# A gated attention unit with a token mixer: the small last group projected within a run of large ones, a reordered opening, and an earlier small output at the end

## The chip, the cores and the metric

The kernel runs on one core of a Trainium2 chip. The metric is the device time of one execution in microseconds. A core has TensorE (PE; its weight loads are shown as PEld), VectorE (DVE), ScalarE (ACT), GpSimd (POOL) and SyncE (SP, which here only issues DMAs), and 16 DMA engines that serve the queues of all of them.

## What is computed

Two layers, for 8 batches of 3200 rows; `u` and `v` have 256 columns, `z` has 64.

```
scores = z @ z^T / 3200                     # per batch, 3200 x 3200, symmetric
x      = u * (relu(scores)^2 @ v)           # 3200 x 256
wq, wk = x @ w_q, x @ w_k                   # 3200 x 64 each
mixed  = (wq @ wk^T / 8) @ x                # 3200 x 256
out    = relu(mixed) @ w_out                # 3200 x 256
```

There is no softmax, so `wk^T @ x` (64 x 256, the "heads") can be summed up first and `mixed` is `wq` times it.

## The kernel before

**Tiles and groups.** The 3200 rows of a batch are 25 tiles of 128. They form seven groups of output rows: six large ones of 512 and a small last one of 128 (`LASTG`, index 6). For a group and each of the 25 tiles, `scores` (L265) makes a 128 x 512 block of scores; two blocks form a pair, which takes one buffer of two banks in PSUM. `first_stage` reads the pair with relu and a scale into `g` (ACT L287 or DVE L291), `second_stage` squares `g` into `at` in FP16 (ACT L307 or POOL/DVE L310). `second_product` (L353) multiplies `at` with `v` and accumulates in four banks, `acc00` to `acc11`: half of the group's rows by half of the contraction, so that two matmuls of 64 rows run beside each other. Since the scores are symmetric, some blocks are not made again but transposed by DMA (`tt`, `ttl`; L332).

**Gate and second layer.** When a half of a group is done, `gate` copies one bank (ACT or DVE, L370), adds the other (DVE, L371), which frees the accumulators, and POOL multiplies with `u` (L390). A DMA transposes `x` (L402); `projections` (L419) gives `wq` and `wk`, a DMA transposes `wk` (L438), and `heads` (L457) sums `wk^T @ x` over the seven groups of a batch (`hacc`, on DVE). Then per group `mix` (L485), relu into `rt` (ACT L508 or DVE L510), `proj` (L520, the product with `w_out`: 8 matmuls for a large group, 2 for the small one), `proj_out` (DVE L542 or ACT L547) and a store (SP, L548). This second layer of a batch runs between the accumulations of the next one.

**Two score buffers.** Scores, projections, heads, mixes and output projections all take their PSUM from one pool of two buffers (`ps_tile`). Whoever opens a third waits until the first is read.

**The order.** A planner written into the kernel (L582 to L1055) fixes the order of all instructions. It keeps a clock for PE, DVE, ACT and POOL, adds an assumed duration for each instruction (`give`), decides by them which engine takes a pass (`choose`, `squares`, with the constants `BIAS`, `SPARE`, `MORE`, `LATE`, `UNTIL`), and gives PE the next thing that the clocks allow: an accumulation, a pair of scores, or an "extra" of the second layer. `heads_known` releases the mixes of a batch in three steps, groups 0 and 1, groups 2, 3 and 6, and groups 4 and 5. `use_mix` gathers large groups in twos (`PAIRED`) before it asks for a projection; the small group asks for one of its own.

**The opening** is by hand (L988 to L1015): POOL makes the identity, SP and ACT load `z` of batch 0 in four pieces (`ZCH`: 4, 6, 7 and 8 tiles), 28 matmuls on the identity fill PE's first microseconds, three pieces are cast to FP16 twice over (two engines each), turned on PE (L132) and copied to `zT` (L139); POOL loads four pieces of `v`. The fourth piece of `z` is cast on DVE when the planner's clock stands at 8.6 and turned at 10.0. Up to 24 us on that clock pairs may be split into halves on two engines (`UNTIL`).

**The end** (L1102 to L1135) finishes the last batch: seven output projections, of which the small one comes last, its store behind those of group 5.

Of the kernel before, what the change touches and what calls it, by code (L numbers as in the profile page):

```python
# [16 lines left out]
def kernel(  # L17
# [95 lines left out]
    def cast_first(c):  # L113
        n0, nn = ZCH[c]
        casts = [
            (nc.vector.tensor_copy, nc.scalar.copy),
            (nc.scalar.copy, nc.gpsimd.tensor_copy),
            (nc.gpsimd.tensor_copy, nc.vector.tensor_copy),
            (nc.vector.tensor_copy, nc.vector.tensor_copy),
        ][c]  # L120
        for half, cast in enumerate(casts):
            cast(out=zd0[:, n0 : n0 + nn, half, :], in_=z32[n0][:])

    def turn_first(c):
        n0, nn = ZCH[c]
        if c < 3:
            tp = acc_tile((c + 1) // 2 % 2, c % 2, "ztp", FP16)
        else:
            open_slot()
            tp = pps.tile([P, 4 * W], FP16, tag="ps", name="ztp")  # L130
        for i in range(nn):
            nc.tensor.transpose(  # L132
                tp[:, ts(i, P)], zd0[:, n0 + i, :, :].rearrange("p a k -> p (a k)"), ident
            )
        clock[PE] += 0.055 * cold() * nn
        ready = clock[PE] + FROM_PE
        on_act = max(clock[ACT], ready) < max(clock[DVE], ready)
        copy = nc.scalar.copy if on_act else nc.vector.tensor_copy
        copy(out=zT[0][:, ds(n0 * P, nn * P)], in_=tp[:, 0 : nn * P])  # L139
        z_at[c] = give(ACT if on_act else DVE, ready, 0.16 + 0.07 * nn)  # L140
        if c == 3:
            close_slot(z_at[c])

    def warm(n):
        for _ in range(n):
            nc.tensor.matmul(out=idle[:, 0:P], lhsT=ident[:], rhs=ident[:], start=True, stop=True)
# [113 lines left out]
    def scores(p):  # L260
        assert len(ztimes) >= 4 * tiles[2 * p + 1][0] and p_chunk(p) in z_at, (p, clock, len(ztimes), z_at)
        sc = ps_tile("sc")
        for h, (b, gi, ti) in enumerate(tiles[2 * p : 2 * p + 2]):
            gs, gw = starts[gi], widths[gi]
            nc.tensor.matmul(  # L265
                out=sc[:, h, 0:gw],
# [13 lines left out]
    def first_stage(p, sc, ways):  # L280
# [4 lines left out]
        for (hs, w), on_act in zip(parts, ways * 2):  # L285
            if on_act:
                nc.scalar.activation(  # L287
                    out=g[:, hs, 0:w], in_=sc[:, hs, 0:w], func=RELU, scale=GSCALE
                )
            else:  # L290
                nc.vector.tensor_scalar(  # L291
                    out=g[:, hs, 0:w], in0=sc[:, hs, 0:w], scalar1=0.0,
# [235 lines left out]
    def proj_out(b, gi, banks, ways, stores=None, at=0):  # L528
# [3 lines left out]
        else:  # L532
            fo = pg.tile([P, 2, W], FP32, tag="fo", name="fo", bufs=2)
# [64 lines left out]
    PAIRED = [0, 1, 2, 3, 4, 5]  # L598
# [48 lines left out]
    def cold():  # L647
        return 2.0 if clock[PE] < 8.4 else 1.0
# [3 lines left out]
    UNTIL = 24.0  # L652
# [8 lines left out]

    def use_pair():
# [7 lines left out]
        if clock[PE] < UNTIL and max(a + 0.57, d + 0.68) + SPLIT < min(a + 1.03, d + 1.2):  # L670
            ways = [a < d, a >= d]
            done = max(give(ACT, ready, 0.57), give(DVE, ready, 0.68))
        else:
            ways = [choose(a, d)]
            done = give(ACT, ready, 1.03) if ways[0] else give(DVE, ready, 1.2)
# [4 lines left out]
    def squares():  # L680
        while pending and pending[0][0] <= clock[PE] + 0.3:
# [6 lines left out]
            if clock[PE] < UNTIL and max(a + 0.57, c + 0.97) + SPLIT < min(a + 1.06, c + 1.9):  # L688
                ways = [a < c, a >= c]
                done = max(give(ACT, ready, 0.57), give(POOL, ready, 0.97))  # L690
# [78 lines left out]
    def heads_known(b):  # L769
        t = clock[PE]  # L770
        for i, gis in enumerate(([0, 1], [2, 3, LASTG], [4, 5])):
# [3 lines left out]
    def use_mix(b, gi):  # L775
# [14 lines left out]
        if gi in PAIRED:  # L790
            if len(mixed_at) == 2:
                add_extra(done + 0.5, "proj", use_projs)
        else:
            add_extra(done + 0.5, "proj", use_projs)

    def use_projs():
        some = mixed_at[:]
        mixed_at.clear()
        banks = []
        clock[PE] += 0.22  # L800
        for _, b, gi in some:
# [4 lines left out]
            banks.append((b, gi, ps, clock[PE] + FROM_PE))  # L806
        for i, (b, gi, ps, ready) in enumerate(banks):
            project_out(b, gi, ps, ready)

    def project_out(b, gi, ps, ready):  # L810
# [6 lines left out]
        stored.append(1e9)  # L817

        def landed(t, i=len(stored) - 1):
            stored[i] = t  # L820
# [9 lines left out]
    V0 = 56  # L830
    V1 = 11

    def batch_begun(b, t):
        if b + 1 < B:
            t0 = max(t + 6, Z0)
            if b == 0:
                nc.gpsimd.memset(zn[:, 0 : NT + 2 : NT + 1, :], 0.0)
# [32 lines left out]
    SPARE = 0.3  # L870
    MORE = 3.0
    BIAS = 0.2
    XDUE = 5.0
    XWAIT = 2.0
    LATE = 0.3
# [92 lines left out]
    def calm_for(kind):  # L968
# [7 lines left out]
        if kind == "proj":  # L976
            n = len(mixed_at)
# [21 lines left out]
    clock[:] = [4.4, 4.75, 4.3, 7.0]  # L999
    for t, n0, nn in ((7.0, 0, 4), (18.0, 4, 8), (10.5, 12, 6), (14.0, 18, 7)):  # L1000
# [20 lines left out]
    while groups or work or current["left"]:  # L1021
# [10 lines left out]
                and (x[1] != "proj" or all(t + 2.0 <= now for t in stored[-2:][: len(mixed_at)]))  # L1032
# [5 lines left out]
        if extra and extra[1] == "proj":  # L1038
            room = slots[len(mixed_at) - 1] <= now
# [84 lines left out]
    for gi in range(NG):  # L1124
# [3 lines left out]
        elif gi == LASTG - 1:  # L1128
            mixed(last, LASTG, LASTG)
        if gi == 0:  # L1130
# [3 lines left out]
        else:  # L1134
            projected(last, gi, [(True, nc.sync, widths[gi] // P)])  # L1135
# [30 lines left out]
```

## Time and profile before

| | us |
|---|---|
| runs of the kernel before | 777.76, 778.35, 779.88 (median 778.35) |
| the profiled execution | 776.21 |
| its span in the trace | 774.4 |
| PE busy in it | 762.9 (99%) |
| DVE, ACT, POOL busy | 518.8, 548.5, 603.2 |

A row of a group gives the line, the engine, the operation, what is written from what, the count, then after the bar the busy time in us and the mean of one in ns, and after the second bar the idle time in front of it with its releasers. A row of the timeline begins with start and duration in us; a number in brackets is the idle time ahead of it. A row of the windows gives the stretch, then busy time and count for PE, PEld, DVE, ACT and POOL, the granted clock, the DMA engines' busy share and GB/s. A row of waits gives who waited for whom, the total in us, how often, and the longest. A row of DMA issues gives the size and the microseconds from issue to landing.

### The profile page before, as it was taken

Reading aid. Unit: us, or ns where it says so; the run is one execution under the profiler, and the core shown is the slowest. Engines: PE = TensorE matmul, PEld = TensorE weight load, DVE = VectorE, ACT = ScalarE, POOL = GpSimd, SP = SyncE. Lnnn points to the kernel's source line nnn. Section 1 sums busy time; section 2 is a strip of 40 time slices with the busy share of each in tenths; the row PEclk is TensorE's granted clock in tenths of the full one; section 3 lists DMA queues with packets and bytes.
Section 4 is the critical chain, followed back from the end, with each engine's and each line's share of the span. In section 5 each row is a group of like instructions: output and inputs, shape, how many; then the busy total and the mean of one; then the engine's idle time right before and its main releaser. Section 6 shows DMA issues by size and latency. Waiting matters only on the chain.

```text
span 774.4 us, 28287 instructions
## 1 busy us (share of the span) xinstructions
PE 762.9 (99%) x12410; PEld 673.8 (87%) x12410; DVE 518.8 (67%) x550; ACT 548.5 (71%) x635; POOL 603.2 (78%) x510
## 2 busy tenths in 40 slices
PE   7999999999999999999999999999999999999996
PEld 6889999889898888988889888998889988898884
DVE  6687687766676566766667657675676756765545
ACT  6686777577666677776877767787587777677734
POOL 7789688888787679867879878778866778878941
PEclk9999999999999999999999999999999999999999
DMA  7999999999999979999999988999999998889745
GB/s 184 157 167 184 133 191 164 169 196 200 187 219 186 198 200 189 174 188 185 207 186 185 201 199 149 198 171 174 229 195 189 161 237 168 162 176 206 144 91 190
DMA packets 307115, 141.10 MB, mean 182 GB/s; under 512 B 285744, under 2 KB 288432, under 8 KB 306992
## 3 DMA queue, kind: packets, MB, share of 16 engines
q1 hardware_dynamic: 300224, 123.13, 82.6%
q0 software_dynamic: 6624, 15.98, 14.8%
q8 instruction: 97, 1.59, 0.9%
q10 hardware_dynamic: 144, 0.20, 0.1%
q14 instruction: 26, 0.21, 0.1%
HBM read 59.64 MB, written 26.21 MB: 111 GB/s over the span
## 4 chain that ended last, share of the span: by engine, by line
PE 94%; DVE 2%; DMA 2%; POOL 1%; issue 0%; ACT 0%; POOLq 0%; DVEq 0%; SPq 0%
PE acc L353 69%; PE sc L265 13%; PE fo L520 6%; PE qk L419 3%; PE qk L457 2%; PE mx L485 1%; DMA v_sb<-in_v_dram 1%; DVE g L291 1%; POOL x_sb L390 1%; DMA z<-in_z_dram 0%; DVE fo L542 0%; DMA xT_sb<-x_sb 0%; DVE both L371 0%; POOL at L310 0%; DVE both L370 0%
## 5 line engine op out<-in xcount | busy, mean ns | idle before, releaser
L353 PE MATMUL acc<-v_sb,at 64*128 64x256 f16 x7344 | 500.8, 269 | 1.3 <-POOL at L310 0.8
L310 POOL TENSOR_TENSOR at<-g 128x1024 f16<-128x1024 f32 (+2 forms) x232 | 414.4, 1799 | 84.8 <-DVE g L291 46.3
L353 PEld LDWEIGHTS <-at 64*128 64x128 f16 x7344 | 403.1, 94 | 52.8 <-issue 7.2
L291 DVE TENSOR_SCALAR g<-sc 128x1024 f32<-128x1024 f32 (+1 forms) x294 | 341.2, 1181 | 107.5 <-PE sc L265 97.4
L307 ACT ACTIVATE at<-g 128x1024 f16<-128x1024 f32 (+1 forms) x250 | 251.3, 1021 | 27.3 <-DVE g L291 24.1
L287 ACT ACTIVATE g<-sc 128x1024 f32<-128x1024 f32 (+2 forms) x184 | 180.5, 984 | 76.6 <-PE sc L265 72.0
L265 PE MATMUL sc<-zT 64*128 64x512 f16 x924 | 186.5, 375 | 2.4 <-DVE g L291 1.4
L390 POOL TENSOR_TENSOR x_sb<-both,u_sb 128x512 f16<-128x512 f32 (+1 forms) x112 | 135.6, 1215 | 63.7 <-DVE both L371 62.9
L353 PE MATMUL acc<-v_sb,tt 64*128 64x256 f16 x2272 | 162.7, 269 | 0.0
L353 PEld LDWEIGHTS <-tt 64*128 64x128 f16 x2272 | 126.6, 94 | 11.1
L371 DVE TENSOR_TENSOR both<-acc,both 128x512 f32<-128x512 f32 (+1 forms) x104 | 69.7, 671 | 23.6 <-ACT both L370 18.7
L265 PEld LDWEIGHTS <-zT 64*128 64x128 f16 x924 | 61.9, 94 | 7.9 <-issue 4.0
L370 ACT COPY both<-acc 128x512 f32<-128x512 f32 (+1 forms) x63 | 36.0, 571 | 45.7 <-PE acc L353 41.8
L542 DVE TENSOR_SCALAR fo<-fo 128x1024 f32<-128x1024 f32 (+2 forms) x30 | 33.1, 1116 | 42.7 <-PE fo L520 42.6
L508 ACT ACTIVATE rt<-mx 128x1024 f16<-128x1024 f32 (+1 forms) x46 | 42.5, 926 | 12.8 <-PE mx L485 12.7
L520 PE MATMUL fo<-wo,rt 128*128 128x256 f16 x400 | 49.5, 274 | 0.1
L370 DVE COPY both<-acc 128x512 f32<-128x512 f32 (+1 forms) x41 | 27.3, 665 | 31.3 <-PE acc L353 28.5
L520 PEld LDWEIGHTS <-rt 128*128 128x128 f16 x400 | 36.4, 98 | 10.7 <-issue 6.5
L433 ACT CAST qk<-qk 128x512 f16<-128x512 f32 (+1 forms) x45 | 24.4, 542 | 25.3 <-PE qk L457 22.7
L547 ACT ACTIVATE fo<-fo 128x1024 f32<-128x1024 f32 (+2 forms) x28 | 24.4, 871 | 23.7 <-PE fo L520 23.0
L472 DVE TENSOR_TENSOR ha<-qk,ha 128x512 f32<-128x512 f32 x37 | 25.5, 688 | 16.7 <-ACT qk L433 16.2
L419 PE MATMUL qk<-xT_sb,wqk 64*128 64x256 f16 (+1 forms) x404 | 32.8, 266 | 0.0
(47 smaller groups left out, 276.4 us busy)
## 6 DMA issues: line engine op xcount, KB each, us to landing
u_sb<-in_u_dram SPq DMA_DIRECT2D x48, 512.0 KB, 4.7
out_dram<-fo SPq DMA_DIRECT2D x46, 512.0 KB, 4.2
v_sb<-in_v_dram POOLq DMA_DIRECT2D x35, 320.0 KB, 6.1
zn<-in_z_dram POOLq DMA_DIRECT2D x7, 400.0 KB, 5.9
tt<-at SPq DMA_TRANSPOSE x143, 4.5
u_sb<-in_u_dram SPq DMA_DIRECT2D x8, 128.0 KB, 3.0
out_dram<-fo SPq DMA_DIRECT2D x8, 128.0 KB, 3.5
out_dram<-fo SPq DMA_DIRECT2D x4, 256.0 KB, 2.6
```

The costliest lines, as they stand in the source:

```text
L265: nc.tensor.matmul(out=sc[:, h, 0:gw], lhsT=z_cols(b, h, ti * P, P), rhs=z_cols(b, h, gs, gw), start=True, stop=True,)
L287: nc.scalar.activation(out=g[:, hs, 0:w], in_=sc[:, hs, 0:w], func=RELU, scale=GSCALE)
L291: nc.vector.tensor_scalar(out=g[:, hs, 0:w], in0=sc[:, hs, 0:w], scalar1=0.0, scalar2=GSCALE, op0=AOP.max, op1=AOP.mult,)
L307: nc.scalar.square(out=out, in_=g[:, hs, 0:w])
L310: mul(out=out, in0=g[:, hs, 0:w], in1=g[:, hs, 0:w])
L353: nc.tensor.matmul(out=accs[half, r][:, ds((j % 2) * D, D)], lhsT=weights(b, gi, ti, j)[top(r), :], rhs=vs[b][top(r), ti, :], start=(first ...
L370: copy(out=both[:, 0 : n * D], in_=accs[half, 0][:, 0 : n * D])
L371: nc.vector.tensor_add(out=both[:, 0 : n * D], in0=accs[half, 1][:, 0 : n * D], in1=both[:, 0 : n * D])
L390: nc.gpsimd.tensor_mul(out=xs[b, gi][:, 0:n, :, r, :].rearrange("p n c d -> p (n c) d"), in0=both[:, 0 : n * D].rearrange("p (m d) -> p m ...
L419: nc.tensor.matmul(out=ps[:, r, 0 : n * P], lhsT=wqk[top(r), c, :, :].rearrange("p t h -> p (t h)"), rhs=xTs[b, gi][top(r), 0:n, c, :], st ...
L508: nc.scalar.activation(out=out, in_=part, func=RELU)
L520: nc.tensor.matmul(out=banks[r][:, ds(j * D, D)], lhsT=flat[:, ds((dc * n + j) * P, P)], rhs=wo[:, dc, :], start=(dc == 0 and j == 0), sto ...
```

## The change

Four things change.

1. **Runs of projections.** `RUNS` replaces `PAIRED`: groups 2, 3 and 6 are mixed and then projected in one go, the small group first. Its relu result and its output get small buffers of their own (`rtl`, `fol`), the sum of heads has one buffer instead of two, and the store of the small output no longer counts among those that hold the next projection back. Each output is read right behind its own projection in the order.
2. **The opening.** DVE clears the later home of `w_out` and the two padding tiles of `z`; the first matmuls run on that cleared tile (31 instead of 28, and none later). POOL asks for the first piece of `v` ahead of the identity and for the second right behind it. All four pieces of `z` are cast at once, the fourth by POOL and ACT; it is turned at 7.5 on the planner's clock. The first pair of scores goes to two accumulator banks (`first_pair`), split on ACT and DVE, and squared by ACT and POOL. The fourth piece of `v` is asked for at 7.5.
3. **The planner's constants.** Score passes are never split any more, squares only before 8 us; `SPARE` 0.3 to 0.1, `MORE` 3.0 to 0.6, `BIAS` 0.2 to -0.2, `XWAIT` 2 to 7, `LATE` 0.3 to 0.5, `V0` 56 to 48, `V1` 11 to 10. A smaller `MORE` lets DVE take squares, a negative `BIAS` prefers ACT for score passes and outputs.
4. **The end.** The small group is projected and stored ahead of group 5, its output read by ACT.

```diff
 def cast_first(c):
-            (nc.vector.tensor_copy, nc.vector.tensor_copy),
+            (nc.gpsimd.tensor_copy, nc.scalar.copy),
...
 def heads_out(b, gi, ps):
-            hacc[b] = psml.tile([P, 2, D], FP32, tag="ha", name="ha")
+            hacc[b] = psml.tile([P, 2, D], FP32, tag="ha", name="ha", bufs=1)
...
 def mix_out(b, gi, ps, by_act=True):
-            rts[b, gi] = prt.tile([P, 2, ND, HW], FP16, tag="rt", name="rt")
+            if gi < LASTG:
+                rts[b, gi] = prt.tile([P, 2, ND, HW], FP16, tag="rt", name="rt")
+            else:
+                rts[b, gi] = prt.tile([P, 1, ND, P], FP16, tag="rtl", name="rtl", bufs=1)
...
-    PAIRED = [0, 1, 2, 3, 4, 5]
+    RUNS = [[0, 1], [2, 3, LASTG], [4, 5]]
...
+    def first_pair():
+        produced[0] += 1
+        sc = scores(0, [acc_tile(0, r, "sc")[:] for r in range(2)])
+        clock[PE] += 0.22
+        ready = clock[PE] + FROM_PE
+        a, d = give(ACT, ready, 0.6), give(DVE, ready, 0.69)
+        free_at[0] = max(a, d)
+        g = first_stage(0, sc, [True, False])
+        for x, t in zip(tiles, (give(ACT, a, 0.63), give(POOL, d, 1.05))):
+            row_at[x] = t + 0.3
...
 def use_mix(b, gi):
-        if gi in PAIRED:
-            if len(mixed_at) == 2:
-                add_extra(done + 0.5, "proj", use_projs)
-        else:
+        if len(mixed_at) == len(next(x for x in RUNS if gi in x)):
             add_extra(done + 0.5, "proj", use_projs)

 def use_projs():
-        some = mixed_at[:]
+        some = sorted(mixed_at[:], key=lambda x: (x[2] < LASTG, x[2]))
...
-            banks.append((b, gi, ps, clock[PE] + FROM_PE))
-        for i, (b, gi, ps, ready) in enumerate(banks):
-            project_out(b, gi, ps, ready)
+            project_out(b, gi, ps, clock[PE] + FROM_PE)
...
-    make_identity(nc, ident)
+    blank = wo[:, 0, 0:P]
+    nc.vector.memset(blank, 0.0)
+    nc.vector.memset(zn[:, 0 : NT + 2 : NT + 1, :], 0.0)
     load_first_z()
     load_first_v(0, 4)
-    idle = acc_tile(0, 1, "warm")
-    warm(28)
-    cast_first(0)
-    cast_first(1)
-    cast_first(2)
+    make_identity(nc, ident)
     load_first_v(12, 6)
+    idle = acc_tile(1, 0, "warm")
+    warm(31)
+    for c in range(4):
+        cast_first(c)
     load_first_v(18, 7)
-    load_first_v(4, 8)
...
-    use_pair()
+    first_pair()
     use_pair()
     turn_first(2)
-    warm(5)
-    at_time(8.6, lambda: (cast_first(3), give(DVE, 8.6, 0.86)))
-    at_time(10.0, lambda: turn_first(3))
+    at_time(T3, lambda: turn_first(3))
+    at_time(V3, lambda: (load_first_v(4, 8), give(POOL, clock[PE], 0.6)))
...
-    for gi in range(NG):
+    for gi in range(LASTG):
...
         elif gi == LASTG - 1:
             mixed(last, LASTG, LASTG)
+            projected(last, LASTG, [(False, nc.sync, 1)])
```

More of the change, by code (lines that the diff above doesn't have):

```diff
@@ L136, in turn_first @@
         ready = clock[PE] + FROM_PE
-        on_act = max(clock[ACT], ready) < max(clock[DVE], ready)
-        copy = nc.scalar.copy if on_act else nc.vector.tensor_copy
+        ways = [(max(clock[e], ready) + t, e, t) for e, t in ((DVE, 0.16 + 0.066 * nn), (ACT, 0.17 + 0.105 * nn))]
+        _, engine, t = min(ways)
+        copy = nc.scalar.copy if engine == ACT else nc.vector.tensor_copy
         copy(out=zT[0][:, ds(n0 * P, nn * P)], in_=tp[:, 0 : nn * P])
-        z_at[c] = give(ACT if on_act else DVE, ready, 0.16 + 0.07 * nn)
-        if c == 3:
-            close_slot(z_at[c])
+        z_at[c] = give(engine, ready, t)
+        free_at[1] = max(free_at.get(1, 0.0), z_at[c])
     def warm(n):
         for _ in range(n):
-            nc.tensor.matmul(out=idle[:, 0:P], lhsT=ident[:], rhs=ident[:], start=True, stop=True)
+            nc.tensor.matmul(out=idle[:, 0:P], lhsT=blank, rhs=blank, start=True, stop=True)
         clock[PE] += 0.053 * cold() * n
@@ L669, in use_pair @@
         a, d = (max(clock[x], ready) for x in (ACT, DVE))
[L670 to L675, printed above, removed]
+        ways = [choose(a, d)]
+        done = give(ACT, ready, 1.03) if ways[0] else give(DVE, ready, 1.22)
         g = first_stage(p, sc, ways)
```

74 lines of the change are left out of this document (39 added, 35 removed).

## The prediction

> **What bounds the kernel now.** I read the page's busy shares first, then the windows by stage, then TensorE's own waits. Every number is of one profiled execution: 776.21 us, of which the span is 774.4; the median of the three runs shown is 778.35, so 2.14 us is put on top of a sum made against the profiled execution. A change of less than 0.3% (2.3 us) can hardly be told from none here; that is the bound of "same" below.
>
> ```profile
> span 774.4 us, 28287 instructions
> PE 762.9 (99%) x12410; PEld 673.8 (87%) x12410; DVE 518.8 (67%) x550; ACT 548.5 (71%) x635; POOL 603.2 (78%) x510
> ...
> 4.50:8.70 4.20, 2.83 (x33) 1.82 (x33) 3.47 (x6) 2.93 (x6) 4.16 (x7) 1.00 0.88 203
> 8.70:16.00 7.30, 5.99 (x90) 4.61 (x91) 6.15 (x9) 4.69 (x8) 5.75 (x5) 1.00 1.03 237
> 16.00:24.00 8.00, 7.49 (x117) 6.04 (x113) 6.09 (x8) 6.62 (x13) 7.10 (x7) 1.00 0.60 93
> 50.00:60.00 10.00, 9.10 (x146) 8.01 (x144) 8.59 (x9) 8.82 (x11) 8.15 (x9) 1.00 1.00 148
> 60.00:100.00 40.00, 40.00 (x687) 39.08 (x684) 28.37 (x31) 27.70 (x31) 32.31 (x29) 1.00 1.08 163
> ```
>
> TensorE is busy for 99% of the span, and busy time flatters it, since overlapping matmuls count as busy however slowly they are issued. The count in brackets shows the pace: from 60 to 100 us 687 matmuls start in 40 us, 17.2 per us. At that pace the 90 of 8.7 to 16 us are 5.2 us of work (2.1 lost), the 117 of 16 to 24 us are 6.8 (1.2 lost), the 146 of 50 to 60 us are 8.5 (1.5 lost). So apart from its fixed work this kernel can be made faster only in the opening, in the patch around 50 us, in the changes of matmul kind, and behind the last matmul.
>
> ```profile
> PE sc L265 <- DVE g L291: 1.4, 3, 0.7
> PE acc L353 <- POOL at L310: 0.8, 1, 0.8
> PE acc L353 <- DVE both L371: 0.2, 1, 0.2
> PEld L520 <- issue: 6.5, 31, 0.2
> ```
>
> TensorE's waits for other engines are few and short; the weight loads of the output projection (L520) stand idle 0.2 us on entry 31 times, whatever else goes on.
>
> **Part 1: the small group inside a run of two.** Before, each of the seven scheduled batches visits the output projection four times (16, 16, 2 and 16 matmuls); after, three times (16, 18, 16), as the changed program's instruction order shows: 28 entries become 21, with 400 matmuls in both. One small visit:
>
> ```profile
> L353 PE MATMUL acc<-v_sb,at 64*128 64x256 f16 x7344 | 500.8, 269 | 1.3 <-POOL at L310 0.8
> ...
> 188.45 1.42 PE L353 MATMUL acc<-v_sb,ttl 64*128 64x256 f16 x22
> 189.80 0.11 PEld L520 LDWEIGHTS <-rt 128*128 128x128 f16 x2 [0.21 <-issue]
> 189.80 0.39 PE L520 MATMUL fo<-wo,rt 128*128 128x256 f16 x2
> 190.13 0.83 PE L353 MATMUL acc<-v_sb,ttl 64*128 64x256 f16 x12
> ```
>
> The 22 accumulations take 1.42 us; without the last one's 0.269 that is 1.15 for 21 starts, 55 ns each. The last of them thus starts at 189.60, and the next accumulation at 190.13: 0.53 us. Had the two projections (128 rows and the same 256 columns, so twice 55 ns) stood in a longer run, they would add 0.22 and the step between two accumulations 0.055. The visit itself costs the rest, 0.25 us. Seven of them are 1.7 us saved (1.75, rounded down for the reading of hundredths). TensorE is the bound, so this is not hidden by anything, and it can hardly be more.
>
> The price: the run opens three score buffers out of two, so the second large projection waits until the small result has been read. From the small one's first matmul to the second large one pass 2 + 8 projection matmuls, about 1.07 us; the read takes 0.385 on ACT (row below), with 0.21 for its matmuls and some 0.3 of handing over: 0.9. It is hidden if ACT is free, and costs up to one square (1.06) if ACT has one in hand. Between 0 and 7 x 0.9 = 6.3 us; six of the seven stand on ACT behind a square or a score pass placed well ahead, so I take 0.4 us in all. The own small buffers (for the relu result, the output and the single copy of the head sum) are reused a batch, some 90 us, later: nothing.
>
> ```profile
> L291 DVE TENSOR_SCALAR g<-sc 128x1024 f32<-128x1024 f32 x276 | 331.7, 1221 | 101.6 <-PE sc L265 94.0 <-POOL at L310 3.6 <-POOL kx L450 1.9
> L287 ACT ACTIVATE g<-sc 128x1024 f32<-128x1024 f32 x170 | 173.5, 1022 | 70.0 <-PE sc L265 69.4
> L307 ACT ACTIVATE at<-g 128x1024 f16<-128x1024 f32 x232 | 242.0, 1056 | 27.3 <-DVE g L291 24.1
> L310 POOL TENSOR_TENSOR at<-g 128x1024 f16<-128x1024 f32 x210 | 394.9, 1892 | 81.6 <-DVE g L291 43.2 <-ACT g L287 25.8 <-DMA tt<-at 5.7
> L291 DVE TENSOR_SCALAR g<-sc 128x512 f32<-128x512 f32 x13 | 8.7, 685 | 3.9 <-ACT g L287 2.6 <-PE sc L265 1.2
> L287 ACT ACTIVATE g<-sc 128x512 f32<-128x512 f32 x11 | 6.6, 596 | 6.6 <-DVE g L291 3.9 <-PE sc L265 2.6
> L310 POOL TENSOR_TENSOR at<-g 128x512 f16<-128x512 f32 x17 | 17.7, 1056 | 1.7 <-DVE g L291 1.6
> L307 ACT ACTIVATE at<-g 128x512 f16<-128x512 f32 x15 | 9.1, 627 | 0.0
> L547 ACT ACTIVATE fo<-fo 128x256 f32<-128x256 f32 x6 | 2.3, 385 | 1.4 <-PE fo L520 1.4
> ```
>
> **Part 2: the opening.** What happens now, and what its chain of waits names:
>
> ```profile
> 0.75 1.35 SPq L108 DMA_DIRECT2D z<-in_z_dram  x3
> 3.85 1.10 DVE L122 CAST zd<-z 128x256 f16<-128x256 f32 x2 [3.85 <-DMA z<-in_z_dram]
> 5.03 0.89 DVE L139 COPY zT<-ztp 128x512 f16<-128x512 f16 x2
> 5.51 0.61 PE L265 MATMUL sc<-zT 64*128 64x512 f16 x4 [0.18 <-DVE zT L139]
> 5.94 1.51 ACT L287 ACTIVATE g<-sc 128x512 f32<-128x512 f32 x2 [1.27 <-PE sc L265]
> 8.69 0.83 PE L353 MATMUL acc<-v_sb,at 64*128 64x256 f16 x12 [0.76 <-POOL at L310]
> 10.54 0.62 PE L132 MATMUL ztp<-ident,zd 128*128 128x128 f16 x8 [0.70 <-DVE zd L122]
> ...
> 4.87 7.83 DMA v_sb<-in_v_dram
> ...
> z<-in_z_dram SPq DMA_DIRECT2D x1, 256.0 KB, 6.8
> z<-in_z_dram SPq DMA_DIRECT2D x1, 224.0 KB, 3.1
> ```
>
> The accumulation begins at 8.69 and waits again for the second piece of v, which POOL asks for at 4.87, after its casts. In the change POOL asks for the first piece before the identity and for the second behind it, some 2.5 us sooner; that wait should go. The warming matmuls run on a tile that DVE clears instead of the identity, and so start sooner; the first scores stay near 5.5 all the same, because DVE's two casts and two copies (1.10 and 0.89) set them. The fourth piece of z is cast at once, one half on ACT and one on POOL, and turned before any accumulation; whole pairs replace split halves after 8 us.
>
> With the row times and the changed order: ACT's half of the first pair (0.60) 5.94 to 6.54 and its square (0.63) to 7.2; a copy of turned z (896 wide, so 0.9 between ACT's rows for 512 and 1024) to 8.1; then in turn scores (1.02) and squares to 9.2, 9.8, 10.8, 11.9, 12.9. DVE: half a pair (0.69) to 6.7, a whole one (1.22) to 7.9, a copy to 8.6, scores to 9.8 and 11.6. POOL: a half square (1.06) to 7.8, the last v request, a half to 9.4, whole ones (1.89) to 11.3 and 13.2. On TensorE the first accumulation stands behind the fourth pair's scores, which need the buffer that DVE frees at 7.9: it starts at 8.2. Then buffers make it wait 0.35, 0.24, 0.35, 0.16 and 0.42 until about 13, and hardly afterwards. By 18.4 us 173 matmuls are done in place of some 154; 19 at 17.2 per us are 1.1 us. Of what is lost from there to 24 us I give it another 0.3: 1.4 us saved, with 0 and 3.3 (all that the two windows lose) as bounds, if the fourth piece of z is there by about 5.5. Whether it is stays open: the last of SP's three requests, which end at 2.1, it is made at about 1.7 and took 6.8 us here; the 224 KB piece ahead of it took 3.1. As nothing waited for it before, its lateness cost nothing; the first rival is about that.
>
> **Part 3: the planner's new constants** reorder the whole program. The loss near 50 us comes from scores that waited for a buffer (1.4 and its neighbours above). In the new order the tightest reuse of a score buffer there is gone, but one gate near 30 us follows closer. Of 1.5 us I count 0.7 saved; bounds 1.5 saved and 0.8 lost.
>
> The constants also put 49 whole squares on DVE, which has none before. ACT gets 69 more whole score passes and 20 more outputs and gives up 24 squares and 12 relu passes, all near 1.02 to 1.06: 53 us more, 602. POOL gives up 15 whole and 12 half squares: 41 less, 562. DVE gives up 62 score passes and 20 outputs for 12 relu passes and the 49 squares, all taken at 1.22: 26 less, 493. None lies above POOL's 603 of now, so no engine becomes the bound. But a square on DVE reads two SBUF operands. The trace has such operations beside POOL:
>
> ```profile
> 751.78 0.69 DVE L379 TENSOR_TENSOR xd<-both,u_sb 128x512 f16<-128x512 f32 x1
> 751.82 1.78 POOL L390 TENSOR_TENSOR x_sb<-both,u_sb 128x512 f16<-128x512 f32 x1 [10.01 <-DVE both L371]
> ...
> L390 POOL TENSOR_TENSOR x_sb<-both,u_sb 128x512 f16<-128x512 f32 x96 | 124.1, 1294 | 56.9 <-DVE both L371 56.0 <-PE acc L353 0.4
> ```
>
> POOL's product took 1.78 where its mean is 1.29: 0.5 longer beside a DVE product of 0.69. A square twice as wide would hold POOL up by about 1.0, and if POOL began first I expect the converse, DVE held up by as much as one POOL square (1.89). The Trainium skill, "SBUF — State Buffer", section "SBUF: two separate sides", says that a VectorE operation with two SBUF inputs and a GpSimd operation reading SBUF lock each other out for a whole instruction, whichever starts first; the row agrees for VectorE first, and no run here shows the other order for such a product. 49 x 1.0 = 49 us on POOL fits into its idle time, so on the path I count 0.5 us; bounds 0 and the second rival's price.
>
> **Part 4: the end.** The small output moves ahead of the last large one.
>
> ```profile
> 766.00:772.50 6.50, 2.92 (x25) 1.97 (x22) 3.76 (x5) 2.36 (x5) 0.00 (x0) 1.00 1.00 403
> ```
>
> From 766 to 772.5 the DMA engines are full with the outputs at 403 GB/s. The same bytes go out in another order: 0, give or take 0.3.
>
> **Sum:** -1.7 + 0.4 - 1.4 - 0.7 + 0.5 + 0 = -2.9 us: 773.3 for a profiled execution, 775.4 for the median.
>
> **Rivals.** *The fourth z piece is late again.* If it lands at 1.7 + 6.8 = 8.5, ACT and POOL stand behind it with their casts; ACT's first scores move from 5.9 to 9.1, POOL's half square ends at 10.7, and the accumulation starts at 10.7 instead of 8.2. That gives back 2.5: 777.9. For it: the row of 6.8. Against: the piece ahead of it came in 3.1, and v's requests fall at other times.
>
> *DVE and POOL lock each other out on the path (slower).* In the changed order 24 of the DVE squares stand directly ahead of a gate's copy or sum, which frees the accumulators for the next group. A square held up by half of a POOL square at POOL's 78% is 0.74 late; the next group's first matmul leaves about 0.4 of slack, so 24 x 0.34 = 8.2 instead of 0.5: 783.1. It decides from 0.14 us per gate (no gain left), and from 0.24 the kernel is slower by 0.3%. For it: the 1.78 row. Against: TensorE now waits for a gate once, for 0.2.
>
> *The run of three doesn't pay.* ACT has a square in hand at most small results, 0.8 each: 7 x 0.8 = 5.6 in place of 0.4: 780.6.
>
> **How the numbers follow.** Forecast 0.50, late z 0.22, lock 0.20, run of three 0.08. The forecast's own range is 772.0 (opening and the patch near 50 us at two thirds of their bounds) to 777.5; faster by over 0.3% means below 776.0, which is most of it (0.42) and a little of the late z (0.03). Slower means above 780.7: the lock and most of the run of three, 0.26. The rest, 0.29, is same. A range from 772.0 to 781.5 leaves out about 0.05 below and 0.15 above.
>
> **What would show it.** Entries into the projection with 0.2 idle: 24 instead of 31. First accumulation near 8.2; ACT's first scores near 5.9 (right) or 9 (late z). Over 165 matmuls between 50 and 60 us. In TensorE's waits, lines for the small result's reader or for the gates above 2 us, or POOL squares well over 1.9 and DVE squares well over 1.3, would make it wrong.

## The result, and the profile after

| | before | after |
|---|---|---|
| median (lowest to highest), us | 778.06 (776.82 to 780.12) | 783.5 (782.29 to 785.16) |
| profiled execution, us | 776.21 | 782.53 |
| its span, us | 774.4 | 780.8 |

The ratio is 1.0076, 95% interval 1.0061 to 1.0091: the change makes the kernel 5.4 us slower. The forecast was 775.4, with 781.5 as the upper end of its range.

The page of the changed kernel: the span and the engines' busy time, then the groups of the squares, on GpSimd and on VectorE (busy us, mean ns, idle time before them).

```profile
span 780.8 us, 28231 instructions
PE 763.7 (98%) x12408; PEld 673.3 (86%) x12408; DVE 526.1 (67%) x518; ACT 586.4 (75%) x680; POOL 595.3 (76%) x481
...
L307 POOL TENSOR_TENSOR at<-g 128x1024 f16<-128x1024 f32 (+1 forms) x203 | 385.6, 1910 | 85.1 <-DVE g L288 60.8
L307 DVE TENSOR_TENSOR at<-g 128x1024 f16<-128x1024 f32 (+2 forms) x53 | 102.5, 1941 | 8.1 <-ACT g L284 7.3
```

No engine is fuller than TensorE, as forecast. But a square on VectorE, counted in the prediction at 1.22 us, takes 1.94 in the mean (2.00 for the 49 of full width), a little longer than the same square on GpSimd (1.91, and 1.95 at full width), and the waits stand there too.

TensorE's waits, and those of its weight loads at the output projection:

```profile
PE acc L350 <- DVE both L368: 3.6, 4, 1.8
PE sc L261 <- DVE g L288: 2.9, 3, 2.1
PE qk L416 <- DVE g L288: 1.6, 1, 1.6
PE fo L520 <- ACT rt L504: 0.5, 1, 0.5
PEld L520 <- issue: 5.2, 25, 0.2
```

Before, the longest wait in the list was 1.4 us, at the warming matmuls; a gate (`both`) cost 0.2 once. Now three of VectorE's steps behind a square each hold TensorE for 1.6 to 2.1 us. The last row is the forecast one: 25 entries with 0.2 idle in place of 31 (24 were forecast).

The windows that were shown of before (TensorE's busy time, and the number of matmuls in brackets, come first):

```profile
4.50:8.70 4.20, 3.73 (x41) 2.10 (x42) 4.17 (x7) 2.52 (x5) 2.76 (x5) 1.00 1.05 251
8.70:16.00 7.30, 6.37 (x94) 4.90 (x92) 4.59 (x5) 7.30 (x10) 7.28 (x6) 1.00 1.02 240
16.00:24.00 8.00, 7.99 (x133) 6.98 (x130) 6.75 (x7) 7.11 (x8) 7.48 (x4) 1.00 0.48 90
50.00:60.00 10.00, 10.00 (x172) 9.13 (x170) 7.94 (x9) 9.40 (x10) 9.76 (x8) 1.00 1.24 172
60.00:100.00 40.00, 38.87 (x663) 36.62 (x659) 27.37 (x28) 27.00 (x31) 31.59 (x29) 1.00 1.10 172
```

The opening and the patch near 50 us are better, as meant: 133 matmuls for 117 in 16 to 24 us, 172 for 146 in 50 to 60. The steady stretch is worse: 663 for 687 in 60 to 100.

To place the time over a whole run I took each trace's matmuls at TensorE's own pace (consecutive accumulations start 54 ns apart in the median) and call what a stretch takes beyond that lost. All numbers are us, from the profiled executions:

| kernel | 0 to 24 | 24 to 60 | 60 to 740 | from 740 | all, against before |
|---|---|---|---|---|---|
| before | 10.1 | 2.8 | 22.1 | 8.2 | |
| after | 8.2 | 2.1 | 30.6 | 8.7 | +6.3 |
| after, GpSimd's squares as two fills (below) | 9.1 | 1.6 | 20.8 | 8.0 | -3.7 |
| after, VectorE's squares with one operand | 10.6 | 2.3 | 21.2 | 8.2 | -0.8 |
| after, no squares on VectorE | 10.6 | 1.4 | 26.5 | 8.4 | +3.7 |
| before, with squares on VectorE | 10.5 | 3.5 | 33.6 | 8.7 | +13.1 |

The loss lies between 60 and 740 us (8.5, and 0.5 behind it); the first 60 us are 2.6 better. In the long stretch the trace of after has eight gaps of 0.40 to 2.47 us between starts of matmuls, 10.0 us together; before has none as long. Seven of the eight lie during or right behind a VectorE square of 2.5 to 4.4 us. The longest, in the timeline (start, duration, engine, operation, count; in brackets the idle time before and who ended it):

```profile
556.97 5.59 POOL L307 TENSOR_TENSOR at<-g 128x1024 f16<-128x1024 f32 x3
...
559.42 4.22 DVE L307 TENSOR_TENSOR at<-g 128x1024 f16<-128x1024 f32 x1
...
562.50 1.51 POOL L447 COPY kx<-kx 128x128 f16<-128x128 f16 x2
563.56 1.21 DVE L288 TENSOR_SCALAR g<-sc 128x1024 f32<-128x1024 f32 x1
...
564.83 0.39 PE L261 MATMUL sc<-zT 64*128 64x512 f16 x2 [2.10 <-DVE g L288]
```

GpSimd does three squares in a row, each in its usual time. VectorE's square is taken up inside the second of them, gets its turn only when the third is over (562.56), and ends 4.22 us after its start. The score pass behind it on VectorE starts at 563.56, and TensorE, which needs that score buffer, has waited 2.10 us.

### The profile page after: what moved, and what is told of

Read it like the earlier page. It is cut to its first block, busy times and chain, and to the rows that moved or that the text cites. A ratio compares the mean times of both kernels' runs of the same rounds, so it can differ in the third digit from the quotient of the medians.

```text
span 780.8 us, 28231 instructions
## 1 busy us (share of the span) xinstructions
PE 763.7 (98%) x12408; PEld 673.3 (86%) x12408; DVE 526.1 (67%) x518; ACT 586.4 (75%) x680; POOL 595.3 (76%) x481
## 4 chain that ended last, share of the span: by engine, by line
PE 90%; DVE 4%; issue 2%; ACT 2%; POOL 1%; DMA 1%; POOLq 0%; SPq 0%; DVEq 0%; ACTq 0%
PE acc L350 65%; PE sc L261 12%; PE fo L520 6%; PE qk L416 3%; PE qk L454 2%; DVE at L307 2%; PE mx L482 1%; DVE g L288 1%; ACT g L284 1%; DMA z<-in_z_dram 1%; DVE both L368 1%; POOL x_sb L387 1%; ACT at L304 0%; POOL at L307 0%; DMA xT_sb<-x_sb 0%
## 5 line engine op out<-in xcount | busy, mean ns | idle before, releaser
L307 POOL TENSOR_TENSOR at<-g 128x1024 f16<-128x1024 f32 (+1 forms) x203 | 385.6, 1910 | 85.1 <-DVE g L288 60.8
L288 DVE TENSOR_SCALAR g<-sc 128x1024 f32<-128x1024 f32 (+2 forms) x219 | 261.7, 1205 | 133.5 <-PE sc L261 129.6
L284 ACT ACTIVATE g<-sc 128x1024 f32<-128x1024 f32 (+2 forms) x252 | 247.0, 993 | 71.1 <-PE sc L261 68.6
L304 ACT ACTIVATE at<-g 128x1024 f16<-128x1024 f32 (+2 forms) x216 | 219.7, 1037 | 11.8 <-DVE g L288 9.7
L387 POOL TENSOR_TENSOR x_sb<-both,u_sb 128x512 f16<-128x512 f32 (+1 forms) x112 | 145.2, 1302 | 80.9 <-DVE both L368 78.6
L307 DVE TENSOR_TENSOR at<-g 128x1024 f16<-128x1024 f32 (+2 forms) x53 | 102.5, 1941 | 8.1 <-ACT g L284 7.3
L261 PEld LDWEIGHTS <-zT 64*128 64x128 f16 x924 | 60.8, 94 | 10.8 <-issue 6.8
L550 ACT ACTIVATE fo<-fo 128x1024 f32<-128x1024 f32 (+2 forms) x43 | 40.9, 996 | 22.8 <-PE fo L520 22.7
L520 PE MATMUL fo<-wo,rt 128*128 128x256 f16 x386 | 46.8, 273 | 0.5 <-ACT rt L504 0.5
L520 PEld LDWEIGHTS <-rt 128*128 128x128 f16 x386 | 36.2, 98 | 8.6 <-issue 3.8
L447 POOL COPY kx<-kx 128x128 f16<-128x128 f16 (+1 forms) x99 | 36.5, 398 | 0.0
L508 ACT ACTIVATE rt<-mx 128x1024 f16<-128x1024 f32 x27 | 27.6, 1021 | 9.2 <-PE mx L482 9.1
```

The source lines that it names most:

```text
L261: nc.tensor.matmul(out=sc[h][:, 0:gw] if banks else sc[:, h, 0:gw], lhsT=z_cols(b, h, ti * P, P), rhs=z_cols(b, h, gs, gw), start=True, st ...
L284: nc.scalar.activation(out=g[:, hs, 0:w], in_=part, func=RELU, scale=GSCALE)
L288: nc.vector.tensor_scalar(out=g[:, hs, 0:w], in0=part, scalar1=0.0, scalar2=GSCALE, op0=AOP.max, op1=AOP.mult,)
L304: nc.scalar.square(out=out, in_=g[:, hs, 0:w])
L307: mul(out=out, in0=g[:, hs, 0:w], in1=g[:, hs, 0:w])
L387: nc.gpsimd.tensor_mul(out=xs[b, gi][:, 0:n, :, r, :].rearrange("p n c d -> p (n c) d"), in0=both[:, 0 : n * D].rearrange("p (m d) -> p m ...
```

## The experiments

**1. Without squares on VectorE, and those squares alone.** In the changed kernel the planner's bar for them is set out of reach; in the kernel before, the new bar alone is put in (53 squares there too). Either gives another planned order.

```
 a_nodve (after):  -    MORE = 0.6    +    MORE = 1e6
 b_dve (before):   -    MORE = 3.0    +    MORE = 0.6
```

> The changed kernel with MORE so large that DVE takes no squares; the planner then lays the order out anew with squares on ACT and POOL alone. Lock theory (DVE squares, locked out by POOL's products, hold back the gates and score passes behind them): TensorE's waits above 0.4 us between 60 and 740 us go, some 9 us, and the time falls to 773 to 776, below the kernel before. Rival (the other constants or the runs of three make TensorE wait): it stays at 781 or above. Second rival (ACT and POOL are short of time without DVE's help): new waits for ACT or POOL, 780 to 784.

> The kernel before with MORE at 0.6 alone, which puts some 53 squares on DVE. Lock theory: DVE squares of 1.9 us in the mean, up to 4, and 5 to 10 us slower than before (783 to 788). Rival (DVE squares are harmless, the other constants do it): within 1.5 us of 778.

Measured: without them 777.92 us, ratio to before 1.0004 [0.9986, 1.0021], so 5.6 us below after; with them alone 789.86, ratio 1.015 [1.012, 1.0179]. TensorE's waits in the second, then its page:

```profile
PE acc L353 <- DMA v_sb<-in_v_dram: 6.6, 3, 5.4
PE sc L265 <- DVE g L291: 3.9, 5, 2.1
```

```profile
L310 DVE TENSOR_TENSOR at<-g 128x1024 f16<-128x1024 f32 x53 | 85.1, 1606 | 3.6 <-ACT g L287 2.4
```

Both point to the squares, and both miss their forecast. The first was to reach 773 to 776; it still loses 26.5 us between 60 and 740, with five gaps of 0.5 to 2.1 us of its new order. The second was to take 783 to 788 with a mean of 1.9; it takes more with a mean of 1.61, but 5.4 us of its profile is one late piece of v, which has no shown link to the squares. So the planner's orders don't give the lock's price; an unchanged order has to.

**2. The same order without the lock.** GpSimd's squares become fills of the same tile, first one (0.94 us), then two (as long as a square).

```
-                mul = nc.vector.tensor_mul if on_act else nc.gpsimd.tensor_mul
+                if on_act: nc.vector.tensor_mul(out=out, in0=g[:, hs, 0:w], in1=g[:, hs, 0:w])
+                else: nc.gpsimd.memset(out, 0.5)      # a_poolset; twice in a_poolset2
```

> The changed kernel in the same order, but POOL writes a constant where it squares, so it reads nothing from SBUF there (the squares of those pairs are left out of the result). Lock theory: DVE squares that begin beside such a write last 1.2 to 1.4 us, their mean falls from 1.94 to about 1.4 (POOL's product with u and its copies still read), and most long waits of TensorE go. Rival (a DVE square of this shape is long by itself or waits for its operand): the mean stays near 1.9.

> The changed kernel with GpSimd's squares replaced by two fills of the same tile with a constant (the product is left out, so the output is another); one fill took 0.94 us, so GpSimd is held as long as by a square, but reads nothing from SBUF. In the order of instructions nothing else moves. If the lock between VectorE's and GpSimd's products is what costs: VectorE's squares stay at 1.25 us, the stalls above 1 us of TensorE between 60 and 740 us are gone, and the time is some 9 us below the changed kernel (773 to 775). If the earlier gain of the single fill came from GpSimd's halved work instead: TensorE waits for GpSimd's tiles again, and the time is 779 or more.

Measured: one fill 773.31 us in its one execution (after: 782.53), with VectorE's squares of full width at 1.30 in the mean. Two fills 775.16, ratio 0.9954 [0.9928, 0.9981], 8.3 us below after. The page of the second:

```profile
L310 POOL MEMSET at<- 128x1024 f16 (+2 forms) x406 | 372.0, 930 | 11.7
...
L307 DVE TENSOR_TENSOR at<-g 128x1024 f16<-128x1024 f32 (+2 forms) x53 | 66.9, 1268 | 12.2 <-ACT g L284 8.4
```

GpSimd is held for 372 us, nearly the 386 of its squares, and the kernel with one fill, half as long, loses the same 20.8 us between 60 and 740 us; so it is not less work for GpSimd that helps. VectorE's squares fall from 1.94 to 1.27, no gap over 0.3 us is left between 60 and 740, and the loss there falls from 30.6 to 20.8. With the rest unchanged and in the same order, that puts the lock's price at 9.8 us in this pair of traces. One more thing differs: a fill need not wait for a score pass, as the squares did (idle time ahead of them 11.7 us in place of 85.1). The next experiment keeps that wait.

**3. One operand in place of two on VectorE.**

```
-                mul(out=out, in0=g[:, hs, 0:w], in1=g[:, hs, 0:w])        # on VectorE
+                nc.vector.tensor_scalar(out=out, in0=g[:, hs, 0:w], scalar1=0.0, scalar2=0.5, op0=AOP.max, op1=AOP.mult)
```

> The changed kernel with VectorE's squares replaced by a relu and scaling of the same tile to the same tile (one SBUF operand in place of two; the squaring is left out for those tiles). If it takes two SBUF operands on VectorE to be held up by GpSimd: mean near 1.2 us or less, and 773 to 776 us. If any VectorE work that reads SBUF is held up: mean near 1.9 us as in the changed kernel, and 782 or more.

Measured: 775.82, ratio 0.9969 [0.9947, 0.9991]. The time is as expected, the reason is not:

```profile
L309 POOL TENSOR_TENSOR at<-g 128x1024 f16<-128x1024 f32 x195 | 370.0, 1906 | 92.0 <-DVE g L288 66.6 <-ACT g L284 13.1 <-issue 9.6
...
L307 DVE TENSOR_SCALAR at<-g 128x1024 f16<-128x1024 f32 x49 | 65.8, 1344 | 11.6 <-ACT g L284 10.8
```

The shortest of these takes 0.68 us, the mean is 1.34, the longest 4.62. So an operation with one SBUF operand is held up too; it only stays near the 1.22 that the planner reckons with because it is so much shorter. The Trainium skill, "SBUF — State Buffer", section "SBUF: two separate sides", counts VectorE's two-port mode among the operations that take the lock. That fits if this operation runs in that mode, as its 0.68 us against 1.22 for the product suggests; no view here names the mode, and my expectation had left it out.

GpSimd's squares and their waits for score passes are as in the changed kernel here (92.0 us idle), and yet the loss between 60 and 740 us is 21.2, about as with the fills. So it was not the fills' freedom from that wait that helped. This run alone could not tell a shorter operation from a lock, and the fills alone could not tell the lock from that wait; what the two share is that VectorE is done sooner.

**4. The lock by itself.** Ahead of the kernel before, GpSimd does n products in a row and VectorE one, begun some 0.3 us into the first; then the other way round; then VectorE reads PSUM, or one SBUF operand.

```
+        for n in (0, 1, 2, 3, 4, 6):
+            nc.gpsimd.memset(fl[:, 0:1], 0.0)
+            for i in range(n): nc.gpsimd.tensor_mul(out=oa[i % 3][:], in0=ga[:], in1=ga[:])
+            nc.scalar.copy(out=pt[:, 0:1], in_=fl[:, 0:1])
+            nc.vector.tensor_copy(out=fl[:, 2:3], in_=pt[:, 0:1])
+            nc.vector.tensor_mul(out=ob[:], in0=gb[:], in1=gb[:])
```

> The kernel before with a test ahead of its first instruction (its own time is not of interest): GpSimd does 0, 1, 2, 3, 4, 6 products of 128x1024 in a row (1.89 us each), and VectorE begins one product (1.22 us alone) about half a microsecond into the first. If the loser waits until the other engine has a gap, VectorE's product takes about 1.2, 2.6, 4.5, 6.4, 8.2, 12 us. If the lock passes on after each instruction, it takes 1.2 and then 2.6 in all the other cases. Then the other way round, VectorE 1, 2, 4 products in a row and one of GpSimd begun inside the first: 2.5, 3.7, 6.1 us if GpSimd starves in the same way, 2.5 to 3 in all cases if not. Last, VectorE reads PSUM (0.69 us) or one SBUF operand (1.2 us or less) beside three products of GpSimd: not held up, if it takes two SBUF operands.

From the timeline, in order of time: VectorE's product (L1001) for n = 0, 1, 2 and 6, with GpSimd's (L1007) for n = 1 and 2; one GpSimd product beside two of VectorE (L1021); VectorE's read of PSUM (L1032) and of one SBUF operand (L1034):

```profile
5.26 1.22 DVE L1001 TENSOR_TENSOR ob<-tb 128x1024 f16<-128x1024 f32 x1
...
7.20 1.89 POOL L1007 TENSOR_TENSOR oa<-ta 128x1024 f16<-128x1024 f32 x1
...
7.46 2.71 DVE L1001 TENSOR_TENSOR ob<-tb 128x1024 f16<-128x1024 f32 x1
...
10.87 4.72 POOL L1007 TENSOR_TENSOR oa<-ta 128x1024 f16<-128x1024 f32 x2
...
11.21 2.63 DVE L1001 TENSOR_TENSOR ob<-tb 128x1024 f16<-128x1024 f32 x1
...
31.68 2.63 DVE L1001 TENSOR_TENSOR ob<-tb 128x1024 f16<-128x1024 f32 x1
...
48.44 2.88 POOL L1021 TENSOR_TENSOR ob<-tb 128x1024 f16<-128x1024 f32 x1
...
58.65 0.68 DVE L1032 TENSOR_SCALAR tb<-pt 128x512 f32<-128x512 f32 x1
...
64.49 2.10 DVE L1034 TENSOR_SCALAR ob<-tb 128x1024 f16<-128x1024 f32 x1
```

VectorE loses to the instruction in hand and no more: 2.63 for n = 2 as for n = 6. GpSimd's next product then waits in its turn (4.72 for two in place of 3.78, and 2.88 in place of 1.89 the other way round). A read of PSUM is not held up (0.68); a read of one SBUF operand is (2.10). So here the lock passes on after each instruction, and a square was held up by 1.5 us at most (2.71 - 1.22). In the changed kernel 48 of 53 are no longer than that allows: at most 2.91, with 3.11 for one GpSimd square (1.89) and their own 1.22. Five are longer (3.51, 3.62, 4.22 and 4.40 us, and 2.63 at half the width, which takes 0.68 alone): VectorE lost to two or three GpSimd instructions in a row.

**5. Shorter instructions on GpSimd.** Each whole square there becomes two of half the width, in the same order.

```
+                    for i in range(n):
+                        x = g[:, hs.start + i, 0:w]
+                        nc.gpsimd.tensor_mul(out=out[:, i, :], in0=x, in1=x)
```

> The changed kernel in the same order, but each whole square on GpSimd is two instructions of half the width (1.06 us each in place of one of 1.89). If VectorE loses to the one GpSimd instruction in hand, its wait is at most 1.06 us: mean of its squares 1.6 us in place of 1.94, and the changed kernel's stalls above 1 us become fewer; some 3 to 5 us below the changed kernel, though GpSimd has 40 us more to do (779 to 781). If VectorE waits for a gap on GpSimd, its mean stays at 1.9 or rises, and the time is 783 or more.

Measured: 791.02, ratio 1.0171 [1.0138, 1.0203], 7.5 us above after. A row of its page, then two of its timeline:

```profile
L307 DVE TENSOR_TENSOR at<-g 128x1024 f16<-128x1024 f32 (+2 forms) x53 | 103.6, 1962 | 9.1 <-ACT g L284 8.3
```

```profile
109.97 6.02 POOL L311 TENSOR_TENSOR at<-g 128x512 f16<-128x512 f32 x6
112.55 5.76 DVE L307 TENSOR_TENSOR at<-g 128x1024 f16<-128x1024 f32 x1
```

VectorE's mean didn't fall. GpSimd's squares also came to 36 us more, so the 7.5 us are not the lock's alone. Of GpSimd's six halves in a row, none is lengthened (1.00 each), and VectorE, which stands ready from 112.55, comes in only behind them and a product of 1.26. So in the kernel a row of GpSimd instructions can keep VectorE out for as long as it lasts; in the test of experiment 4 it never did. What makes the difference isn't settled: the operand was ready each time (its writer had ended 0.03 us or more before), and the four longest squares of the changed kernel began at different points of GpSimd's instruction.

**6. The opening alone,** in the kernel before, with and without the two VectorE squares that the planner then makes.

```
 b_open: the diff's opening alone (turn_first, first_pair, warm, the order of the first loads, UNTIL = 8.0)
 b_open_n: the same with    MORE = 1e6
```

> The kernel before with the new opening alone (constants, runs of projections and the end as before). From the traces the new opening has lost 2.0 us less of TensorE's time by 24 us, so 776.0. Rival (what is won at the start is waited for later, for v or for the transposed blocks): 778.

> The kernel before with the new opening alone, as in the run of that part, but without any square on VectorE. If those two squares made that part 0.5% slower, it gains what the forecast gave the opening, 0.8 us or more (ratio 0.999 or less), when the fourth piece of z is there in time, and 0 when it is late. If the opening itself costs, ratio 1.003 or more again.

Measured: 781.23, ratio 1.0051 [1.003, 1.0072], and 782.22, ratio 1.0065 [1.0041, 1.009]; the runs of each spread over 8 us. The first is slower than both values that were expected (776.0 and 778). The ScalarE cast of the fourth piece of z and the first accumulation in the timeline of b_open, with the squares:

```profile
7.87 0.62 ACT L122 CAST zd<-z 128x512 f16<-128x512 f32 x1 [3.45 <-DMA z<-in_z_dram]
9.97 0.64 PE L350 MATMUL acc<-v_sb,at 64*128 64x256 f16 x4
```

In that of b_open_n, without them:

```profile
9.09 0.62 ACT L122 CAST zd<-z 128x512 f16<-128x512 f32 x1 [4.49 <-DMA z<-in_z_dram]
10.92 1.16 PE L350 MATMUL acc<-v_sb,at 64*128 64x256 f16 x9
```

And of the changed kernel:

```profile
6.32 0.62 ACT L122 CAST zd<-z 128x512 f16<-128x512 f32 x1 [1.65 <-DMA z<-in_z_dram]
6.84 0.59 ACT L284 ACTIVATE g<-sc 128x512 f32<-128x512 f32 x1
...
8.15 1.19 PE L350 MATMUL acc<-v_sb,at 64*128 64x256 f16 x12
```

Eight profiles have these same first instructions. The cast starts at 6.32, 7.28, 7.87, 7.93, 8.06, 8.59, 8.68 and 9.09, and the loss up to 24 us goes with it: 8.2, 9.1, 10.6, 10.0, 10.6, 10.6, 10.8 and 13.0, against 10.1 before. The gain of 1.9 in the changed kernel's profile is the best case; from about 8 on there is none. Both single-part kernels lose more elsewhere, by their new order (in b_open gaps of 0.8 to 1.0 us at 22, 28 and 41 us).

**7. The fourth piece handled late again,** in the changed kernel without squares on VectorE; and that kernel with the opening of before.

```
 n_zlate:  cast_first(3) at 8.6 planned us and turn_first(3) at 10.0, through a score buffer;  BIAS = 0.0
 n_bopen:  before, with the new runs, constants and end;  MORE = 1e6
```

> The changed kernel without squares on VectorE and with its own opening, but the fourth piece of z cast at about 8.6 us and turned at about 10, through a score buffer, as before (one constant, BIAS, is 0.0 in place of -0.2). If the late piece costs the opening's gain, ScalarE's first scores start near 5.9 us and the first accumulation near 8.2 in its profile whenever the piece lands, and the time is 1 to 2.5 us below the 777.9 of the changed kernel without squares on VectorE (ratio 0.997 to 0.999). If the order of later work is what costs, ratio 1.000 or more.

> The changed kernel without squares on VectorE and with the opening of before: what is left are the runs, the planner's constants and the end. If the new opening eats its own gain when the fourth piece of z lands late, this stands at the forecast's -1.7 + 0.4 - 0.7 + 0.6 = -1.4 us (ratio 0.998), below the 777.9 us of the changed kernel without squares on VectorE. If instead the new constants' order of scores and squares costs time without any lock, it stays at or above 777.9 (ratio 1.0015 or more).

Measured: 776.80, ratio 0.9986 [0.9975, 0.9997]; and 780.14, ratio 1.0039 [1.0025, 1.0053]. In the first, ScalarE's scores start at 6.12, the first accumulation at 8.25 and the time is 1.1 us below the kernel without squares on VectorE, all as expected. But TensorE then waits for the fourth piece:

```profile
11.04 0.62 PE L132 MATMUL ztp<-ident,zd 128*128 128x128 f16 x8 [1.39 <-POOL zd L122]
```

By 24 us it has lost 10.6, as much as with the piece cast at once; what it gains lies later, between 60 and 740 us, in another planned order. Nor is it shown to be steadier: its 11 runs lie within 1.9 us (5.4 with the piece cast at once), but those of n_best below, with the same late piece, spread over 4.9. The second missed: its order has a cluster of five gaps between 275 and 280 us, 3.9 together, where two mixes stand among narrow score passes.

**8. The run of three alone,** with and without the two VectorE squares that the planner then makes.

```
 b_runs: the diff's RUNS, own small buffers, use_projs and project_out alone
 b_runs_n: the same with    MORE = 1e6    BIAS = 0.15
```

> The kernel before with the runs of the output projection alone changed (two, three with the small one first, two; own small buffers), all else as before. By the forecast's term (28 visits become 21, 0.25 us each, 0.4 given back for the third large one's buffer) 1.3 us below before: ratio 0.998, 24 entries with 0.2 us idle in place of 31. If the run of three doesn't pay (a wait of 0.8 us for the small result in most batches), ratio 1.005 and waits of a large projection for a score buffer in TensorE's list.

> The kernel before with the runs of the output projection alone changed, as in the run of that part, but without any square on VectorE (BIAS is 0.15 in place of 0.2, since the planner does not end with 0.2 here). If its two squares on VectorE were what made that part 0.4% slower, 1.3 us below before (ratio 0.998). If the run of three itself or the new order around it costs, ratio 1.002 or more again.

Measured: 779.63, ratio 1.004 [1.002, 1.0059], and 781.4, ratio 1.0036 [1.0014, 1.0059]. Waits of TensorE and its weight loads in the second:

```profile
PE sc L265 <- DVE g L291: 2.5, 6, 0.7
PE mx L485 <- POOL hs L479: 1.0, 1, 1.0
PEld L523 <- issue: 5.1, 24, 0.3
```

The entries fall to 24 as forecast, and no wait for the small result stands in the list. Yet between 60 and 740 the loss is 24.8 against 22.1: other waits of 0.5 to 1.3 us (scores, a projection, a mix, a piece of v), which before does not have. The squares on VectorE do not explain it, since the second has none. The planner lays out the whole program anew for any edit, and here that moves the time by more than the edit does.

**9. The end alone, and versions meant to be fast.**

```
 b_end: the diff's last loop alone
 n_best: n_zlate with the end of before
 n_best2: n_best with    SPARE = 0.3    BIAS = 0.2    XWAIT = 2.0
```

> The kernel before with the changed end alone: the small group projected and sent ahead of the last large one. The forecast says 0 within 0.3 us. The changed kernel's trace has a wait of 0.69 us of the small projection for its relu result there, which by itself would be ratio 1.0008.

> The changed kernel without squares on VectorE, with the fourth piece of z handled as before (as in the run with the late turn) and with the end of before. The wait of 0.69 us of the small projection at the end goes: 0.5 to 0.7 us below the run with the late turn, 776.1 us, ratio 0.998. If the end is worth nothing, ratio 0.9986 as there.

> The changed kernel without squares on VectorE, with the fourth piece of z handled as before and the end of before, and with three of the planner's constants (SPARE, BIAS, XWAIT) as before. If the constants matter only through the squares on VectorE, it is within 1 us of the same kernel with the new constants (776.6, ratio 0.998); the order is another one, so chance waits of 1 to 3 us in sum can put it on either side of before.

Measured: the end 777.36, ratio 1.001 [0.9994, 1.0026], not to be told from none. The other two 776.56, ratio 0.9978 [0.9955, 1.0002], and 775.38, ratio 0.9979 [0.9956, 1.0002]: 1.0 and 2.1 us below before by the medians, 7 to 8 below after, with intervals that just reach no change. The second's runs fall into two groups (seven of 774.2 to 775.5, five of 778.2 to 779.1); its profile is of the upper one and has one wait of 3.2 us for `xT_sb`'s transposes.

## Why the prediction was wrong

**The step that failed** is the lock's term of part 3. It had the mechanism, with VectorE held up by as much as one GpSimd square, and then counted it on GpSimd's side (1.0 us a square, hidden in its idle time) and put 0.5 us on the path. In the same order with and without the lock it is 9.8. VectorE's side was not worked out: 53 squares x (1.94 - 1.27) = 36 us more, on an engine whose next step can be a gate's sum or a score pass for which TensorE waits. Why a square can lose to a whole row of GpSimd instructions stays open.

**The second rival** was right in mechanism. That its 783.1 lies so near the 783.5 is luck, for the make-up was another: not 24 gates at 0.34, but seven long holds, among them four of the five squares that lost to more than one GpSimd instruction, and score buffers as often as gates. Its reason against, that TensorE waited for a gate only once, was the error: slack against a wait of 0.2 says nothing of one of 2 us. It had 0.20 of the chance; the change's 49 squares had been counted, so the price per square should have decided.

**Part 2, the opening.** In the profile of after, it came much as worked out for a timely piece: first accumulation at 8.15 (forecast 8.2), 1.9 us won by 24 us (forecast 1.4). ScalarE's first scores waited for the piece until 6.84, where 5.9 was forecast. But the first rival, the late piece, is the more frequent case, with the cast at 7.9 or later in six of the eight profiles: cast at 8.6, it gave a first accumulation at 10.5 (that rival: 10.7) and no gain. The row of 6.8 us from request to landing, which I had set against the 3.1 of the piece ahead, was the better witness.

**Part 1, the runs.** Right. From start to start, a visit of two matmuls takes 0.20 us on entry, 0.11 between the two and 0.205 on leaving, 0.52 in all; within a longer run the same two and the step from one accumulation to the next take 0.27. Seven times the difference is 1.7 us, as forecast. Of the 0.4 for the small result 0.2 showed in after's trace, once, near 662 us.

**The patch near 50 us** fell from 2.8 to 2.1 lost between 24 and 60: 0.7, as forecast. **The end** gave 0 within what can be told: its wait of 0.5 us for the fresh relu result (`PE fo L520 <- ACT rt L504` above) is real, but the kernel with the new end alone has it too and loses no more from 740 us on than before (8.2 in both). The 0.5 more of after there is not explained by it.

**The sum** in the profiled pair: -1.9 (opening) - 0.7 (to 60 us) - 1.3 (60 to 740 without the lock: 20.8 for 22.1) + 9.8 (lock) + 0.5 (from 740) = +6.4, the difference of the two spans. Without the lock it would have been -3.4 here, and the forecast without its 0.5 for the lock is -3.4 too. That agreement is partly luck: with the piece of z as late as in most profiles the opening gains nothing.

## What to carry to other kernels

Price a lock between two engines on both sides, and on the side whose next instruction frees something that the bounding engine waits for; busy time that fits into idle time is no argument there. Before moving a product from GpSimd to VectorE, see whether GpSimd runs such products in rows: then the moved one can wait behind several of them (5 of 53 here), and in the mean it took no less time than on GpSimd (2.00 us against 1.95). And where a planner lays out the program, a single-part kernel differs from before by its order too (1 to 4 us here between 60 and 740 us); leave the order and change the instruction instead.

## What the runs showed of the hardware

A VectorE product beside GpSimd products took 2.63 us in place of 1.22, however many of them followed, in the isolated test; in the kernels it could lose to several of them in a row (4.40 us, and 5.76 with halved GpSimd squares), and why is open. GpSimd's fills (0.93 us) did not hold VectorE up, nor did GpSimd hold up VectorE's reads of PSUM (0.68). The fourth piece of z was there for its cast anywhere between 6.3 and 9.1 us with the same first instructions.
